# Full-height products, single PSUM banks, spectra on VectorE and a new order in a fused attention and long-convolution kernel

## The chip, the cores and the metric

The kernel runs on one core of one Trainium2 chip. The metric is device time in microseconds (us), the median of the runs shown. One execution was also taken by the hardware profiler. Its span, from the first instruction to the last, is what the rows below count from. Five engines work beside each other: TensorE (PE for its products, PEld for the loads of its stationary operand), VectorE (DVE), ScalarE (ACT), GpSimd (POOL) and SyncE (SP), which here only issues DMAs.

## What is computed

Two independent results stand side by side in an output of 2,048 rows and 1,152 columns, all in bf16. The left 576 columns are attention with a memory (32 heads of 18), in four segments of 512 rows:

```python
q, k, v = heads(x @ wq), heads(x @ wk), heads(x @ wv)
g = sigmoid(beta)                      # one per head
for s in range(4):                     # segments of 512 rows
    p = softmax(q[s] @ k[s].T * scale + causal_mask)
    a_dot = p @ v[s]
    num = phi(q[s]) @ M                # phi(t) = t + 1 where t > 0, else exp(t)
    den = phi(q[s]) @ z + 1e-6
    out[s] = g * num / den + (1 - g) * a_dot
    M, z = M + phi(k[s]).T @ v[s], z + phi(k[s]).sum(rows)
a = out @ wo
```

The right 576 columns are a gated long convolution of 2,048 taps, which the reference computes by Fourier transforms of 4,096 points:

```python
kv = short_conv(k, shift_k) * v        # 4 taps
y = irfft(rfft(pad(kv)) * rfft(pad(ssm_k)))[:2048]
b = q * (y + kv * ssm_D)
```

## The kernel before

**A list of operations and an order.** The kernel is recorded as a list of operations (`Graph.add`, L75): a name, the engines that could take it, a function that issues its instructions, the buffers that it reads and writes. Three tables at the end of the file then fix everything: `TURN` gives the order in which the operations are issued, `ENGINE` the engine of each, `SLOT` the slot of the pool in which its buffer lies. So on each engine the instructions stand in one order that is written out in full, and an instruction that waits holds all behind it on its engine. The helper `mm` issues TensorE's products (L139 without a position in the array, L141 with one), `copy` the evacuations (L145 on ScalarE, L147 on VectorE). PSUM has 8 banks of 512 fp32 columns; a buffer "ps1" is one bank, "ps2" two neighbours.

**Attention, per segment s.** x is loaded transposed (`x0`: channels 0 to 511 as four blocks of 128, `x4`: channels 448 to 575, so that the last 64 channels lie on rows 64 to 127 of the fifth block), and a copy on chip (`x5`) puts these 64 also on rows 0 to 63. Operations `qk`: for five groups of columns (four of 126, one of 72) and for q and k, four products over 128 channels each; then the last 64 channels of q and of k as two products of 64 rows that run side by side in the upper and the lower half of the array (`tile_position`). Both results lie in one pair of banks and one instruction of 1,024 elements evacuates it (`eqk`). `v` works alike with 288 columns per half, `dq` makes one head group directly in its padded form. Then come scores (L1122, 25 or 18 rows, four row tiles), exponentials on ScalarE (L1129, 1,024 elements each, 160 of them), causal masks on GpSimd (L1136), `av` (32-column tiles), division (L1207, L1208, L1236), the memory term (feature maps `phm` L936, `pha` L948; `nm` L1032), their sum `oo` (L1245, on VectorE or GpSimd) and the output products `out` with `wo` into a pair of banks, evacuated together (576 elements). In the last segment the fourth group of columns (m = 3) is cut at row 54, and its two parts are two products.

**Convolution, in five groups of 64 or 128 channels.** A short convolution by diagonal matrices `dg` (X times dg, into a pair of banks), times v (L433), then a Fourier transform in two stages of small products: `F1` (tiles W and xs, 128 rows by 64 columns, two side by side), `F2` (A and Ft), then the product of the spectra `PP` (L540: X times Hx into PQ, 1,024 elements each, one half of them on VectorE, the other on GpSimd), inverse products `inv` (G and PQ), the evacuation `Z`, a transposing DMA (`zt`, CT from Z), a last stage (`CT,Psi`) and the gate (L595, q).

**The end.** The last scores, the inverse products of channel group 4, its Z copies, their transposing DMA, its last stage and the last output products share the engines at the end of the order.

Of the kernel before, what the change touches and what calls it, by code (L numbers as in the profile page):

```python
# [18 lines left out]
P = 128  # L19
# [10 lines left out]
NDIRECT = 1  # L30
LAT = {"PE": 0.20, "ACT": 0.10, "DVE": 0.10, "POOL": 0.12, "SP": 0.10}
# [10 lines left out]
def c_tt2(n):  # L42
    return 0.16 + n * 0.00054
# [68 lines left out]
class Prog:  # L112
# [138 lines left out]
    def build_b_front(self):  # L251
# [141 lines left out]
        for ct in range(5):  # L393
# [24 lines left out]
            g.add("dg%d" % ct, {"DVE": 0.8, "POOL": 1.2}, dgf, r=[self.ident, self.skf], w=[dg, (kT, 0)], prio=pr - 2)  # L418
            for cp in range(2):
                pc = Buf("ps2", "psconv")  # L420
                for u in range(2):
                    def cm(e, pc=pc, u=u, cp=cp, kT=kT, dg=dg):
                        o = self.ps(pc)
                        c = 2 * cp + u
                        for i in range(4):
                            self.mm(o[:, u, :], self.t(dg)[:, i, :], self.t(kT)[:, 16 + 512 * c - i:16 + 512 * c - i + 512],
                                    i == 0, i == 3)

                    self.pe("conv%d.%d%d" % (ct, cp, u), 2048, 4, cm, [kT, dg], [(pc, u)], pr)

                def ce(e, pc=pc, cp=cp, vT=vT, kv=kv):
                    sl = slice(1024 * cp, 1024 * cp + 1024)
                    self.nc.vector.tensor_tensor(out=self.t(kv)[:, sl], in0=self.psf(pc), in1=self.t(vT)[:, sl], op=ALU.mult)  # L433

                self.evac("kv%d.%d" % (ct, cp), 1024, ce, [pc], [vT], pr, "D")
# [13 lines left out]
    def build_b(self):  # L449
        g, p = self.g, self.p  # L450
        for gi, (c0, Cg) in enumerate(GROUPS):
# [49 lines left out]
            for o in range(16 // KP):  # L501
# [33 lines left out]
                for ri in range(2):  # L535
# [7 lines left out]
                    g.add("PP%d.%d%d" % (gi, o, ri), {"DVE": c_tt2(1024), "POOL": c_pool2(1024)}, pa, r=[Xt, H], w=[(Pt, ri)], prio=to)  # L543
# [63 lines left out]
    def build_a_consts(self):  # L607
# [3 lines left out]
        for nm, src, lead in (("wq", "A_wq", 0), ("wk", "A_wk", 0.1), ("wv", "A_wv", 4), ("wo", "A_wo", 40)):  # L611
# [3 lines left out]
            if nm != "wo":  # L615
                cuts = (0, D) if nm == "wv" else (0, 160, D)
                qs = CQ if nm == "wv" else WQ
                for ci in range(len(cuts) - 1):
                    def l1(e, b=b, src=src, cl=slice(cuts[ci], cuts[ci + 1])):
                        self.q(e).dma_start(out=self.t(b)[:, 0:4, cl], in_=getattr(self, src)[0:512, cl].rearrange("(t p) f -> p t f", p=P))  # L620

                    self.dma(nm + "abc"[ci], l1, [], [(b, "abc"[ci])], pr + 0.3 * ci, 512 * 1152, pk=1152, queues=qs)
                for k in (["q", "k"].index(nm[1]),) if nm != "wv" else (0, 1):
                    fs = slice(288 * k, 288 * k + 288) if nm == "wv" else slice(0, D)

                    def l2(e, b=b, src=src, r=slice(64 - 64 * k, 128 - 64 * k), fs=fs):
                        self.q(e).dma_start(out=self.t(b)[r, 4, fs], in_=getattr(self, src)[512:576, fs])

                    self.dma(nm + "4%d" % k, l2, [], [(b, 1 + k)], pr + 0.2, 64 * 1152, pk=1152, queues=qs)
# [166 lines left out]
    def direct(self, hp, u, pd, xT):  # L796
        pr = self.tA(2 * hp + u) - self.p["lead_pad"] - 2
        pq = Buf("ps2", "psdq")
        for w_ in range(2):
            def dq(e, w_=w_):  # L800
                o = self.ps(pq)
                x = self.t(xT)
                for t in range(4):
                    w = self.t(self.w[("wq", "wk")[w_]])
                    for j in range(4):
                        c = DH * (8 * hp + 4 * u + j)
                        self.mm(o[32 * j:32 * j + 32, w_, :], w[:, t, c:c + 32], x[:, t, :], t == 0, False, (0, 32 * j))
                if w_ == 1:
                    for j in range(4):
                        c = DH * (8 * hp + 4 * u + j)  # L810
                        for i in range(2):
                            r = slice(64 - 64 * i, 128 - 64 * i)
                            w = self.t(self.w[("wq", "wk")[i]])
                            self.mm(o[32 * j:32 * j + 32, i, :], w[r, 4, c:c + 32], x[r, 4, :], False, True, (64 - 64 * i, 32 * j))

            ks = ("a",) if hp == 0 else ("a", "b")
            wt = self.w[("wq", "wk")[w_]]
            self.pe("dq%d.%d%d" % (hp, u, w_), 2560, 20, dq, [(xT, 0)] + [(wt, k) for k in ks] if w_ == 0 else
                    [xT, (self.w["wq"], 1), (self.w["wk"], 2)] + [(wt, k) for k in ks], [(pq, w_)] if w_ == 0 else [pq], pr, al=[pd])
        self.evac("ed%d.%d" % (hp, u), 1024, lambda e: self.copy(e, self.t(pd)[:, u, :, :], self.ps(pq)), [pq], [(pd, u)], pr + 0.5)  # L820

    def build_a(self):
# [18 lines left out]
        g.add("zz", {"POOL": 1.7}, lambda e: self.nc.gpsimd.memset(self.t(zz)[:, 0:1792], 0.0), w=[zz], prio=p["prio_w"] - 40)  # L841
        for i in range(2):
# [9 lines left out]
        for s in range(4):  # L852
# [12 lines left out]
            def lx5(e, xT=xT):  # L865
                self.nc.sync.dma_start(out=self.t(xT)[0:64, 4, :], in_=self.t(xT)[64:128, 4, :])

            self.dma("x4_%d" % s, lx4, [], [(xT, 4)], px, L * 256, pk=4096, issue=0.65, lat=2.2)
            self.dma("x0_%d" % s, lx, [], [(xT, 0)], px + 0.02, L * 1024, pk=4096, issue=0.65, lat=2.2)
            self.dma("x5_%d" % s, lx5, [], [(xT, 4)], px + 0.04, 65536, pk=1024)  # L870
            dense, f = [], []
            for m in range(5):
                M = MS[m]
                pr = ts - p["lead_qk"] + p["d_qk"] * m
                pq = Buf("ps2", "psqk")
                de = Buf("dn", "dense")
                dense.append(de)
                for w_ in range(2):
                    wt = self.w[("wq", "wk")[w_]]

                    def qk(e, pq=pq, w_=w_, wt=wt, m=m, M=M, xT=xT):
                        o = self.ps(pq)
# [555 lines left out]
```

## Time and profile before

| | |
|---|---|
| median of 3 runs | 304.22 us (300.54 to 307.75) |
| profiled execution | 303.91 us |
| span of the profiled execution | 302.2 us |
| mean granted clock of TensorE | 0.98 of full |
| busy: TensorE, VectorE, ScalarE, GpSimd | 268.0, 239.1, 240.1, 183.6 us |

The busy time of TensorE holds its products only. Its products are pipelined: the next may start before the one before has ended, so times of a group are read best from one start to the next. In a row of the timeline the bracket tells how long the engine was idle just before and what ended it. A row "x32" is 32 instructions in a run. The chain that ended last is followed back from the last instruction, at each step to what released it. PEclk, in the windows, is the granted clock as a share of full speed (1.00 is 2.4 GHz, 0.50 is 1.2 GHz).

### The profile page before, as it was taken

The page shows a single profiled execution, that of the slowest core. Times are in us where ns is not written, and L with a number is a line of the kernel's source. Part 1 is how long each engine was busy: PE and PEld are TensorE (multiplying, and loading weights), DVE is VectorE, ACT ScalarE, POOL GpSimd, SP SyncE. Part 2 cuts the span into 40 slices and gives each one's busy share as a digit, 9 for nine tenths or more (in the row PEclk, how much of TensorE's full clock was granted, in tenths as well). Part 3 has the DMA queues.
Part 4 walks back from the last instruction along what each step waited for, and adds up shares of the span by engine and source line. Part 5 has one row for each costly group of instructions (what it writes and reads, how often), then busy time and mean ns, then how long its engine had stood idle before and what let it go on. Part 6 is the DMA issues. An engine that isn't in the chain of part 4 may idle for free.

```text
span 302.2 us, 9484 instructions
## 1 busy us (share of the span) xinstructions
PE 268.0 (89%) x3978; PEld 159.7 (53%) x3978; DVE 239.1 (79%) x334; ACT 240.1 (79%) x270; POOL 183.6 (61%) x196
## 2 busy tenths in 40 slices
PE   2999999978998987999999898999989867877985
PEld 0435565445645554664655475555755534544852
DVE  6896764889999989665989889587978988789541
ACT  3277888989896896879998998889999878986621
POOL 8898043365793495082799934588757498539300
PEclk9999999999999999899999999999999999997798
DMA  8699999999999999468979556295984365783364
GB/s 201 140 184 261 163 210 326 192 205 240 237 177 233 245 128 188 107 162 141 251 153 253 128 164 164 93 230 151 235 166 127 105 171 156 166 205 87 61 96 106
DMA packets 133012, 52.92 MB, mean 175 GB/s; under 512 B 113338, under 2 KB 125738, under 8 KB 132970
## 3 DMA queue, kind: packets, MB, share of 16 engines
q1 hardware_dynamic: 130698, 51.00, 76.7%
q10 hardware_dynamic: 2272, 1.33, 1.7%
q8 instruction: 31, 0.51, 0.7%
q14 instruction: 11, 0.09, 0.1%
HBM read 21.58 MB, written 17.76 MB: 130 GB/s over the span
## 4 chain that ended last, share of the span: by engine, by line
PE 48%; DVE 17%; DMA 15%; ACT 7%; issue 7%; POOL 3%; SPq 2%; ACTq 0%; DVEq 0%; POOLq 0%
PE PS L139 23%; PE PS L141 19%; DMA CT<-Z 8%; ACT P L1129 5%; PE PS L1122 5%; DMA xs<-in_B_ssm_k_dram 4%; DVE Hx L147 2%; POOL P L1136 2%; DVE PQ L540 1%; DMA skb<-in_B_shift_k_dram 1%; DMA pad<-qk_scratch 1%; DVE X L147 1%; DVE Z L147 1%; DVE X L433 1%; DVE xs L326 1%
## 5 line engine op out<-in xcount | busy, mean ns | idle before, releaser
L1129 ACT ACTIVATE P<-PS 128x1024 bf16<-128x1024 f32 x160 | 153.4, 1032 | 24.0 <-PE PS L1122 23.8
L1136 POOL TENSOR_SCALAR_AFFINE_SELECT P<-P 128x512 bf16<-128x512 bf16 (+1 forms) x112 | 82.1, 756 | 70.5 <-ACT P L1129 56.0
L540 POOL TENSOR_TENSOR PQ<-X,Hx 128x1024 bf16<-128x1024 bf16 x18 | 41.0, 2287 | 7.7 <-DVE X L147 6.5
L1122 PE MATMUL PS<-pad 25*128 25x384 bf16 (+6 forms) x512 | 35.6, 302 | 7.6 <-DVE q L595 1.9
L936 POOL TENSOR_SCALAR f<-dn 126x512 bf16<-126x512 bf16 (+1 forms) x9 | 24.7, 2743 | 14.3 <-DVE dn L147 9.5
L139 PE MATMUL PS<-wo,am 126*128 126x288 bf16 (+2 forms) x152 | 24.9, 298 | 1.6 <-POOL am L1245 1.1
L1122 PEld LDWEIGHTS <-pad 25*128 25x128 bf16 (+1 forms) x512 | 11.0, 92 | 28.4 <-issue 23.6
L147 DVE CAST A<-PS 128x1024 bf16<-128x1024 f32 x17 | 20.6, 1216 | 6.4 <-PE PS L141 6.4
L141 PEld LDWEIGHTS <-Ft 128*64 128x64 bf16 x704 | 20.3, 110 | 8.9 <-issue 7.6
L141 PE MATMUL PS<-W,xs 128*64 128x128 bf16 x576 | 22.1, 223 | 2.8 <-ACT P L1129 1.2
L141 PE MATMUL PS<-A,Ft 128*64 128x128 bf16 (+1 forms) x640 | 22.6, 216 | 2.1 <-DVE Hx L147 0.7
L141 PE MATMUL PS<-G,PQ 64*128 64x128 bf16 (+1 forms) x640 | 23.4, 229 | 0.5 <-ACT A L145 0.4
L141 PE MATMUL PS<-P,V 128*32 128x256 bf16 (+3 forms) x512 | 22.9, 302 | 0.5 <-ACT P L1129 0.4
L139 PE MATMUL PS<-xT,wq 128*126 128x512 bf16 (+1 forms) x80 | 22.1, 403 | 1.1 <-DVE X L433 0.6
L147 DVE CAST dn<-PS 126x1024 bf16<-126x1024 f32 (+1 forms) x14 | 17.1, 1218 | 7.4 <-PE PS L141 4.0
L141 PEld LDWEIGHTS <-PQ 64*128 64x128 bf16 (+1 forms) x640 | 20.5, 105 | 4.0 <-issue 2.6
L141 PEld LDWEIGHTS <-xs 128*64 128x64 bf16 x576 | 18.1, 111 | 8.2 <-issue 7.6
L145 ACT CAST A<-PS 128x1024 bf16<-128x1024 f32 x19 | 19.2, 1016 | 3.8 <-PE PS L141 3.5
L139 PE MATMUL PS<-xT,wk 128*126 128x512 bf16 (+1 forms) x80 | 21.4, 390 | 0.0
L540 DVE TENSOR_TENSOR PQ<-X,Hx 128x1024 bf16<-128x1024 bf16 x18 | 21.2, 1186 | 0.0
L139 PE MATMUL PS<-wv,xT 128*128 128x288 bf16 x128 | 20.3, 288 | 0.6 <-ACT P L1129 0.4
L139 PE MATMUL PS<-X,dg 128*128 128x512 bf16 x80 | 19.0, 380 | 0.2 <-DVE pad L147 0.2
(149 smaller groups left out, 474.0 us busy)
## 6 DMA issues: line engine op xcount, KB each, us to landing
pad<-qk_scratch SPq DMA_DIRECT2D x15, 512.0 KB
qk_scratch<-dn SPq DMA_DIRECT2D x16, 252.0 KB
a_scratch<-ou SPq DMA_DIRECT2D x15, 256.0 KB
xs<-in_B_ssm_k_dram SPq DMA_DIRECT2D x4, 512.0 KB
kv_scratch<-X SPq DMA_DIRECT2D x4, 512.0 KB
xs<-kv_scratch SPq DMA_DIRECT2D x4, 512.0 KB
q<-in_B_q_dram SPq DMA_DIRECT2D x8, 256.0 KB
out_dram<-q SPq DMA_DIRECT2D x8, 256.0 KB
```

What stands on the lines that cost most here:

```text
L139: self.nc.tensor.matmul(out, lhsT=lhsT, rhs=rhs, start=start, stop=stop)
L141: self.nc.tensor.matmul(out, lhsT=lhsT, rhs=rhs, start=start, stop=stop, tile_position=pos)
L145: self.nc.scalar.copy(out=out, in_=in_)
L147: self.nc.vector.tensor_copy(out=out, in_=in_)
L326: v.tensor_scalar(out=self.i32(ix), in0=self.i32(it), scalar1=self.t(self.bcol)[:, 0:1], scalar2=self.t(off)[:, 0:1], op0=ALU.mult, op1=AL ...
L433: self.nc.vector.tensor_tensor(out=self.t(kv)[:, sl], in0=self.psf(pc), in1=self.t(vT)[:, sl], op=ALU.mult)
L540: eng.tensor_tensor(out=self.t(Pt)[:, 1024 * ri:1024 * ri + 1024].rearrange("p (b f) -> p b f", b=2), in0=a, in1=self.t(H)[:].rearrange("p ...
L936: eng.tensor_scalar(out=self.t(fm)[0:M, ws, :], in0=self.t(dense[m])[0:M, ws, :], scalar1=0.0, scalar2=1.0, op0=ALU.max, op1=ALU.add)
L1122: nc.tensor.matmul(o, lhsT=t[r, 1, q0:q0 + P], rhs=t[r, 0, q0:L], start=True, stop=True, tile_position=(32 * j, 0))
L1129: self.nc.scalar.activation(out=out2(jj), in_=self.psf(pso[jj]), func=ACT.Exp, scale=scale)
L1136: self.nc.gpsimd.affine_select(out=ap, in_=ap, compare_op=ALU.is_ge, fill=0.0, base=0, pattern=pat + [[1, P]], channel_multiplier=-1)
```

## The change

**Full-height products.** The weights of q, k and v get a fifth block of 128 rows: rows 64 to 127 hold the last 64 channels, rows 0 to 63 are set to zero by a memset (operations `wqz`, `wkz`, `wvz`). A product over that block has 128 rows; what x holds on rows 0 to 63 of its fifth block meets zeros. The pairs of 64-row products go, and so do the copy `x5` and the second loads of the weights' last rows.

```diff
             def lx4(e, xT=xT, s=s):
                 self.nc.sync.dma_start_transpose(out=self.t(xT)[:, 4, :], in_=self.A_x[0, L * s:L * s + L, 448:576])
 
-            def lx5(e, xT=xT):
-                self.nc.sync.dma_start(out=self.t(xT)[0:64, 4, :], in_=self.t(xT)[64:128, 4, :])
-
             self.dma("x4_%d" % s, lx4, [], [(xT, 4)], px, L * 256, pk=4096, issue=0.65, lat=2.2)
             self.dma("x0_%d" % s, lx, [], [(xT, 0)], px + 0.02, L * 1024, pk=4096, issue=0.65, lat=2.2)
-            self.dma("x5_%d" % s, lx5, [], [(xT, 4)], px + 0.04, 65536, pk=1024)
...
+                    def qk(e, pq=pqs[w_], wt=wt, m=m, M=M, xT=xT):
-                        for t in range(4):
-                            self.mm(o[0:M, w_, :], self.t(wt)[:, t, 126 * m:126 * m + M], x[:, t, :], t == 0, False)
-                        if w_ == 1:
-                            for i in range(2):
-                                w = self.t(self.w[("wq", "wk")[i]])
-                                r = slice(64 - 64 * i, 128 - 64 * i)
-                                self.mm(o[0:M, i, :], w[r, 4, 126 * m:126 * m + M], x[r, 4, :], False, True, (64 - 64 * i, 0))
...
+                        for t in range(5):
+                            self.mm(self.psf(pq)[0:M], self.t(wt)[:, t, 126 * m:126 * m + M], x[:, t, :], t == 0, t == 4)
+
+                    self.pe("qk%d.%d%d" % (s, m, w_), 2560, 5, qk, [xT, (wt, 1), (wt, 2)] + [(wt, k) for k in ks], [pqs[w_]], pr, al=[de])
+
+                for w_ in range(2):
+                    def eq(e, pq=pqs[w_], de=de, M=M, w_=w_):
+                        self.copy(e, self.t(de)[0:M, w_, :], self.psf(pq)[0:M])
+
+                    self.evac("eqk%d.%d%d" % (s, m, w_), 512, eq, [pqs[w_]], [(de, w_)], pr + 0.5)
```

The rest of that part, for the weights:

```diff
+                def l2(e, b=b, src=src):
+                    self.q(e).dma_start(out=self.t(b)[64:128, 4, :], in_=getattr(self, src)[512:576, :])
+
+                self.dma(nm + "4", l2, [], [(b, 1)], pr + 0.2, 64 * 1152, pk=1152, queues=WQ if nm != "wv" else CQ)
+                g.add(nm + "z", {"DVE": 0.4, "POOL": 0.7}, lambda e, b=b: (self.nc.vector if e == "DVE" else self.nc.gpsimd).memset(
+                    self.t(b)[0:64, 4, :], 0.0), w=[(b, 2)], prio=pr - 5)
```

**Single banks.** `qk`, `v`, `dq`, the short convolution and `out` write single banks, and each bank has its own evacuation (512 or 288 elements instead of 1,024 or 576). The waits of `phm`, `phe` and the scores name the half that they need.

**Spectra and sums on VectorE.** All 36 products of spectra (now L541), all sums `oo` and the diagonals `dg` are VectorE's. In the last segment `oo` covers m = 3 as well (its 54 rows are added into the memory term), so that the separate output product of 54 rows goes. Five more of the `phm` are GpSimd's (14 instead of 9).

```diff
-                    g.add("PP%d.%d%d" % (gi, o, ri), {"DVE": c_tt2(1024), "POOL": c_pool2(1024)}, pa, r=[Xt, H], w=[(Pt, ri)], prio=to)
+                    g.add("PP%d.%d%d" % (gi, o, ri), {"DVE": c_tt2(1024)}, pa, r=[Xt, H], w=[(Pt, ri)], prio=to)
...
-                if p["o_pool"]:
-                    en["POOL"] = c_pool2(512)
                 if mem:
-                    def o2(e, nb=nm_[s, m], b=am[m], M=M):
-                        eng = self.nc.vector if e == "DVE" else self.nc.gpsimd
-                        eng.tensor_tensor(out=self.t(b)[0:M], in0=self.t(b)[0:M], in1=self.t(nb)[0:M], op=ALU.add)
-
-                    g.add("oo%d.%d" % (s, m), en, o2, r=[nm_[s, m]], w=[am[m]], prio=pr)
+                    back = M < MS[m]
+
+                    def o2(e, nb=nm_[s, m], b=am[m], M=M, to=nm_[s, m] if back else am[m]):
+                        self.nc.vector.tensor_tensor(out=self.t(to)[0:M], in0=self.t(b)[0:M], in1=self.t(nb)[0:M], op=ALU.add)
+
+                    g.add("oo%d.%d" % (s, m), en, o2, r=[am[m] if back else nm_[s, m]], w=[nm_[s, m] if back else am[m]], prio=pr)
...
-                early = early[:3] + [(nm_[s, 3], wo, 3, MS[3]), (nm_[s, 4], wo, 4, MS[4]), (am[3], wo, 3, 54)]
+                early = early[:3] + [(nm_[s, 3], wo, 3, MS[3]), (nm_[s, 4], wo, 4, MS[4])]
```

**Warm-up products.** 18 operations of two products each, 128 rows by 512 columns, whose result nobody reads: identity times a zeroed tile (`warma`, ten), identity times `selb` (`warmb`, eight).

```diff
+        def warm(e, pw, rhs):
+            for i in range(2):
+                self.mm(self.psf(pw), self.t(self.ident)[:], rhs(), True, True)
+
+        for k in range(NWARM[0]):
+            pw = Buf("ps1", "psw")
+            self.pe("warma%d" % k, 1024, 2, lambda e, pw=pw: warm(e, pw, lambda: self.t(zz)[:, 0:512]), [self.ident, zz], [pw], p["prio_w"] - 39)
+        for k in range(NWARM[1]):
+            pw = Buf("ps1", "psw")
+            self.pe("warmb%d" % k, 1024, 2, lambda e, pw=pw: warm(e, pw, lambda: self.t(self.selb)[:, 0, 0:512]), [self.ident, self.selb], [pw],
+                    tA(34))
```

**Order.** `TURN`, `ENGINE` and `SLOT` are new; one line of `TURN`, before and after:

```diff
-    "bQBTAFUAWAAAAIMAbwAfAGwACAABAFQAVgAeAG4ACwAMAAIAVwAcAF4AAwAEAAUACQAgAHIAIwCGAIQAhwBzACEAZQAKAB0AcAAiAFoAWQANAGcABwAOAA8AhQB0AIgAJwAkACUAEAARAH8AjwCQAH"
...
+    "cwAAAHQAiwB5AIoAHAB7AHwAdQB2AGQAXwBgAF0AHgBjAB8AAQAIAAkAAgBhAGIACgALAGoAXgAhAAwAIABnAHgADQBlAIwAZgCnACMAqQClAA4ApgAiAKsAqACOAKoAEgDcAA8AEwCQAJEAEACsAA"
```

By the new tables VectorE evacuates 21 of the 40 `qk` halves (14 of 20 pairs before), 18 of 32 `v` halves (13 of 16 pairs) and 23 of 32 `out` halves (12 of 16 pairs), ScalarE the others. Seven of the warm-up operations stand at TensorE's start, four behind its last output product, seven in between. The weights' columns beyond 160 are loaded from SyncE's queue instead of ScalarE's.

On TensorE, the end of one group of columns of q and k in segment 0 and the short convolution behind it (wq and wk are the weights, xT_113 the transposed x, dg_112 the diagonals, X_0_99 the padded k). Before:

```order
L139 LDWEIGHTS wk
L139 MATMUL PS<-xT_113,wk 126x512
L141 LDWEIGHTS wq
L141 MATMUL PS<-xT_113,wq 126x512
L141 LDWEIGHTS wk
L141 MATMUL PS<-xT_113,wk 126x512
L139 LDWEIGHTS dg_112
```

The two products at L141 are the 64-row pair; ahead of them stand four products at L139 each for q and k. In the new order the fifth block's product of q follows its other four directly, and that of k too (left out are four more pairs of rows of wk):

```order
L140 LDWEIGHTS wq
L140 MATMUL PS<-xT_113,wq 126x512
L140 LDWEIGHTS wk
L140 MATMUL PS<-xT_113,wk 126x512
...
L140 LDWEIGHTS dg_112
L140 MATMUL PS<-X_0_99,dg_112 128x512
```

All rows there have one form, with no change of the array's form between q, k and the convolution.

On VectorE, the end of the work on channel group 4 of the convolution (Hx and X are its spectra, PQ their product, q the gate of group 3, am and nm the two terms of the attention). Before:

```order
L147 CAST Hx_2_107<-PS_63 128x1024
L595 TENSOR_TENSOR q_0_102<-PS_63,q_0_102 128x1024
L540 TENSOR_TENSOR PQ_0_110<-X_1_109,Hx_1_106 128x1024
L595 TENSOR_TENSOR q_0_102<-PS_63,q_0_102 128x1024
L1236 TENSOR_TENSOR am_0_134<-PS_63,am_0_134 126x512
L540 TENSOR_TENSOR PQ_1_111<-X_0_108,Hx_2_107 128x1024
L1032 TENSOR_TENSOR nm_1_141<-PS_63,rd_1_146 126x512
```

After:

```order
L541 TENSOR_TENSOR PQ_1_111<-X_1_109,Hx_0_105 128x1024
L148 CAST oA_1_150<-PS_63 128x288
L148 CAST ou_1_148<-PS_63 128x512
L541 TENSOR_TENSOR PQ_0_110<-X_0_108,Hx_2_107 128x1024
L148 CAST oA_0_149<-PS_63 128x288
L541 TENSOR_TENSOR PQ_1_111<-X_1_109,Hx_0_105 128x1024
L596 TENSOR_TENSOR q_0_102<-PS_63,q_0_102 128x1024
L541 TENSOR_TENSOR PQ_0_110<-X_0_108,Hx_2_107 128x1024
L596 TENSOR_TENSOR q_0_102<-PS_63,q_0_102 128x1024
```

All four products of the group's spectra stand on VectorE, and three of them ahead of the first gate of group 3, where before two stood here and none ahead of it.

On GpSimd, its last instructions (P4 are the exponentials that it masks). Before:

```order
L1136 AFFINE_SELECT P4_2_131<-P4_2_131 128x4x128
L540 TENSOR_TENSOR PQ_0_110<-X_1_109,Hx_1_106 128x1024
L540 TENSOR_TENSOR PQ_1_111<-X_0_108,Hx_2_107 128x1024
L1136 AFFINE_SELECT P4_3_132<-P4_3_132 128x4x128 x2
L1245 TENSOR_TENSOR am_0_134<-am_0_134,nm_2_142 126x512
L1136 AFFINE_SELECT P4_4_133<-P4_4_133 128x4x128
L1245 TENSOR_TENSOR am_1_135<-am_1_135,nm_0_140 126x512
```

After:

```order
L1123 AFFINE_SELECT P4_4_133<-P4_4_133 128x4x128
L1123 AFFINE_SELECT P4_0_129<-P4_0_129 128x4x128 x2
L1123 AFFINE_SELECT P4_1_130<-P4_1_130 128x4x128
L1123 AFFINE_SELECT P4_2_131<-P4_2_131 128x4x128
L1123 AFFINE_SELECT P4_3_132<-P4_3_132 128x8x128
L1123 AFFINE_SELECT P4_4_133<-P4_4_133 128x4x128 x2
```

Only masks are left there: two products of spectra and two sums have moved to VectorE.

## Rows read from the trace of the kernel before

**Rows 1.** Page, part 1: engine, busy us, share of the span, instructions.

```profile
PE 268.0 (89%) x3978; PEld 159.7 (53%) x3978; DVE 239.1 (79%) x334; ACT 240.1 (79%) x270; POOL 183.6 (61%) x196
```

**Rows 2.** Windows: stretch, us, PE, PEld, DVE, ACT, POOL, PEclk, DMA, GB/s.

```profile
20.00:60.00 40.00, 39.13 (x491) 21.66 (x490) 27.93 (x42) 33.74 (x39) 17.09 (x26) 1.00 1.08 234
60.00:240.00 180.00, 166.54 (x2609) 101.17 (x2607) 152.37 (x200) 158.34 (x179) 116.77 (x107) 0.99 0.81 180
240.00:302.20 62.20, 48.33 (x772) 30.84 (x769) 42.58 (x53) 40.70 (x47) 31.90 (x35) 0.93 0.55 127
```

**Rows 3.** Page, part 5: the exponentials of the scores on ScalarE.

```profile
L1129 ACT ACTIVATE P<-PS 128x1024 bf16<-128x1024 f32 x160 | 153.4, 1032 | 24.0 <-PE PS L1122 23.8
```

**Rows 4.** Timeline of TensorE: start us, us, engine line op tile.

```profile
31.81 1.05 PE L139 MATMUL PS<-xT,wk 128*72 128x512 bf16 x4
32.80 0.40 PE L141 MATMUL PS<-xT,wq 64*72 64x512 bf16 x1
32.80 0.40 PE L141 MATMUL PS<-xT,wk 64*72 64x512 bf16 x1
33.13 1.08 PE L141 MATMUL PS<-W,xs 128*64 128x128 bf16 x31
```

**Rows 5.** Timeline of TensorE, GpSimd, ScalarE: the start, [idle before <-releaser].

```profile
5.75 1.90 PE L141 MATMUL PS<-xT,wq 128*32 128x512 bf16 x16 [5.75 <-DMA xT<-in_A_x_dram]
7.58 3.21 PE L139 MATMUL PS<-xT,wq 128*126 128x512 bf16 x8
...
12.43 1.61 POOL L841 MEMSET P<- 128x1792 bf16 x1
...
23.70 1.92 ACT L1129 ACTIVATE P<-PS 128x1024 bf16<-128x1024 f32 x2
```

**Rows 6.** Timeline of VectorE, and one row of GpSimd.

```profile
56.89 0.68 DVE L540 TENSOR_TENSOR PQ<-X,Hx 128x1024 bf16<-128x1024 bf16 x1
57.49 0.68 DVE L147 CAST ou<-PS 128x512 bf16<-128x512 f32 x1
...
65.08 2.36 DVE L540 TENSOR_TENSOR PQ<-X,Hx 128x1024 bf16<-128x1024 bf16 x1
...
154.88 3.63 POOL L936 TENSOR_SCALAR f<-dn 126x1024 bf16<-126x1024 bf16 x1 [0.37 <-DVE dn L147]
...
157.66 0.68 DVE L948 TENSOR_TENSOR f<-f,fe 126x1024 bf16<-126x1024 bf16 x1
```

**Rows 7.** Groups by line and form: busy us, mean ns | idle before.

```profile
L540 POOL TENSOR_TENSOR PQ<-X,Hx 128x1024 bf16<-128x1024 bf16 x18 | 41.0, 2287 | 7.7 <-DVE X L147 6.5 <-PE PS L141 0.9 <-ACT X L145 0.3
...
L540 DVE TENSOR_TENSOR PQ<-X,Hx 128x1024 bf16<-128x1024 bf16 x18 | 21.2, 1186 | 0.0
...
L948 DVE TENSOR_TENSOR f<-f,fe 126x1024 bf16<-126x1024 bf16 x8 | 9.1, 1134 | 0.0
```

**Rows 8.** Timeline of TensorE: three waits.

```profile
118.45 0.62 PE L141 MATMUL PS<-CT,Psi 128*64 128x512 bf16 x4 [2.23 <-DMA CT<-Z]
...
248.13 0.55 PE L139 MATMUL PS<-wo,am 72*128 72x288 bf16 x3 [1.13 <-POOL am L1245]
...
276.78 0.62 PE L1122 MATMUL PS<-pad 25*128 25x512 bf16 x4 [1.94 <-DVE q L595]
```

**Rows 9.** Windows, columns as in rows 2: behind two waits.

```profile
118.50:123.00 4.50, 4.50 (x38) 2.55 (x38) 2.85 (x4) 2.02 (x3) 0.00 (x0) 0.62 0.85 226
276.50:283.20 6.70, 6.42 (x95) 5.26 (x96) 4.54 (x7) 4.43 (x5) 4.63 (x6) 0.50 0.43 81
```

**Rows 10.** Chain that ended last: start us, us, what.

```profile
270.14 0.64 PE PS L141 x4
...
278.01 3.55 PE PS L141 x64
...
286.70 7.34 DMA CT<-Z
...
294.70 3.45 PE PS L139 x22
```

More of the change, by code (lines that the diff above doesn't have):

```diff
@@ L937, in f1 @@
                                                  op0=ALU.max, op1=ALU.add)
-                g.add("phm%d.%d" % (s, m), {"DVE": c_ts4(n), "POOL": c_pool1(n)}, f1, r=[dense[m]], w=[fm], prio=pr)
+                g.add("phm%d.%d" % (s, m), {"DVE": c_ts4(n), "POOL": c_pool1(n)}, f1, r=[(dense[m], k) for k in range(ws.start, ws.stop)], w=[fm], prio=pr)
                 def f2(e, fe=fe, m=m, M=M, ws=ws, dense=dense):
                     self.nc.scalar.activation(out=self.t(fe)[0:M, ws, :], in_=self.t(dense[m])[0:M, ws, :], func=ACT.Exp)
-                g.add("phe%d.%d" % (s, m), {"ACT": c_act(n)}, f2, r=[dense[m]], w=[fe], prio=pr)
+                g.add("phe%d.%d" % (s, m), {"ACT": c_act(n)}, f2, r=[(dense[m], k) for k in range(ws.start, ws.stop)], w=[fe], prio=pr)
                 def f3(e, fm=fm, fe=fe, M=M, ws=ws):
@@ L1125, in score @@
                     cols = sum(L - P * kt for kt, _, _ in which)
-                    g.add(nm, {"PE": cols / 2400.0 + 0.05 * len(which) + 0.03}, sc, r=[(pds, k) for k in sorted({x[2] for x in which})], w=pso, prio=pr, mode="R32", al=[self._pw])
+                    g.add(nm, {"PE": cols / 2400.0 + 0.05 * len(which) + 0.03}, sc, r=[(pds, 2 * k + q) for k in sorted({x[2] for x in which}) for q in range(2)], w=pso, prio=pr, mode="R32", al=[self._pw])
                     for jj in range(2):
@@ L1214, in build_a @@
                 keys = [k for k in splits if k[0] * 4 <= hh]
-                mem = s > 0 and M == MS[m]
+                mem = s > 0
                 K = 16 * keys[-1][1]
@@ L1266, in build_a @@
-                for h in range(2):
-                    self.pe("out%d.%d%d" % (s, tt, h), 1440, 5, lambda e, h=h, op_=op_, ks=early, last=not late: op_(e, h=h, ks=ks, last=last),
-                            [x[0] for x in early] + [wo], [(po, h)], pr, al=[oA])
-                if late:
-                    def fl(e, op_=op_, late=late):
-                        for h in range(2):
-                            op_(e, h=h, ks=late, first=False)
-                    self.pe("outf%d.%d" % (s, tt), 1152, 4, fl, [x[0] for x in late] + [x[1] for x in late], [po], pr + 0.1, al=[oA])
```

214 lines of the change are left out of this document (97 added, 117 removed).

## The prediction

> **What bounds the kernel now.** I read the page's busy shares first, then the same shares by stage, then the costliest groups of instructions with what they wait for, then single stretches of the timeline and, for the end, the chain that ended last. The shares put TensorE first with 89%, VectorE and ScalarE at 79%, GpSimd at 61% [rows 1]. By stage [rows 2]: from 20 to 60 us TensorE is busy 39.1 of 40 us, from 60 to 240 us it is busy 166.5 of 180 (VectorE 152.4, ScalarE 158.3), and in the last 62.2 us only 48.3. So there are three stages: a start in which TensorE has nothing to do for 5.75 us, a long middle in which TensorE paces and the others wait for it (ScalarE's exponentials wait 23.8 us for scores [rows 3]), and an end in which it is idle a fifth of the time. The middle can shorten only if TensorE's own work shrinks or a wait in front of it goes; the end follows its chain of waits.
>
> A busy TensorE is not all products. In the timeline [rows 4] four 512-column products take from 31.81 to 32.80, 0.99 us; at the upper clock, 2.4 GHz, 512 columns are 0.213 us, four are 0.85. The pair of 64-row products behind them, side by side, is 0.213 us of columns and takes until 33.13, 0.33. So each time the array's form changes, 0.12 to 0.14 us pass beyond the columns, a little of it for the products themselves; I take 0.10 us per change. In the program's order on TensorE I count 351 changes of form before.
>
> **The change part by part.**
>
> *Products and forms.* The 64-row pairs become 128-row products. For q and k that is one more product in each of 20 pairs, 20 x 0.213 = 4.3 us; for v 16 x 288 columns (0.120 us) = 1.9; for the directly made head pair 16 products run four instead of eight at once, 0.4. Eight 54-row products of the last output stage go: 8 x 0.120 = -1.0. Sum +5.6. Against that the order has 277 changes instead of 351, and the 54-row products cost two each as well (16): 90 fewer, 90 x 0.10 = -9.0. For q and k alone it is nearly even: a pair with its two changes took 0.33 + 0.1, two full products take 0.43; v gains 0.08 each.
>
> Row tiling for contractions of at most 64 rows is what the Trainium skill recommends (TensorEngine Tiling (Array Packing), When to Use Tiling); by it alone this edit would be a loss of the 6.2 us above for q, k and v. The same page says that a change of mode drains the array (Key Properties) but gives no price. The trace has both: the two halves do start together at 32.80, and the next form starts 0.33 us later, not 0.21.
>
> Of the 18 warm-up pairs, seven stand at the start, four behind the last output product, and seven in the order between: 14 x 0.213 = +3.0 us that count. Products, forms and warm-ups: +5.6 - 9.0 + 3.0 = -0.4; I take 0. If a change cost nothing it would be +8.6; at 0.157 us each, -5.5.
>
> *Start.* Before, the first products wait for the transposed x until 5.75 us, and from 7.58 eight 512-column products then need 3.21 us, 0.40 us each [rows 5]: nearer to the 0.427 us of the lower level, 1.2 GHz, than to 0.213. Now the warm-ups need the zero tile (1.61 us on GpSimd [rows 5]) and the identity, now first on GpSimd, so they may start near 3 us (an estimate) and 14 of them at 0.427 end near 9. By 10.7 us the old kernel has done 12 steps of 512 columns, 2.6 us at full clock; the new one would have 1.7 and no copy of x to wait for. I take 0, from -2 to +2. The weights' zero rows are memsets on an idle VectorE.
>
> *Spectra and additions to VectorE.* 18 products of spectra at 0.60 us (56.89 to the next start at 57.49 [rows 6]) are +10.8 us on VectorE, 8 more additions of 512 elements some 3. What goes is what GpSimd's own two-input products did to it: alone this product takes 0.68 us, at 65.08, beside GpSimd's, 2.36; the 18 have a mean of 1.186 [rows 7], so 18 x 0.51 = 9.1 us go, and the 8 minima of 1,024 (mean 1.134 [rows 7] against 0.68 at 157.66) give 3.6, the rest about 1. VectorE stays even, at about 239 us. Split evacuations (0.68 us for 512 elements, at 57.49) cost a little more in pairs and free a bank sooner. GpSimd loses 18 x 2.29 [rows 7] and seven additions, about 50 us, gets five more feature maps (up to 3.63 us each), and its masks no longer queue behind a 2.3 us product. On the path I see two of these waits: output products at 248.13 wait 1.13 us for GpSimd's addition, and the scores at 276.78 wait 1.94 us for VectorE [rows 8]; the second belongs to the end.
>
> The Trainium skill would have the blocking differently (SBUF — State Buffer, Who interferes with whom): a VectorE instruction with two SBUF inputs contends with any GpSimd instruction that reads SBUF, and the one that came second is blocked throughout. The trace agrees for GpSimd's products, but at 157.66 a minimum took 0.68 us inside a GpSimd feature map of 3.63 us [rows 6]. If the rule decided, the masks, which stay, would block the 36 products: the slower rival below.
>
> *The middle's waits.* The largest is 2.23 us at 118.45, for the transposed spectra of group 0 [rows 8], and the clock falls behind it (0.62 over 118.5 to 123 us [rows 9], 4.5 x 0.38 = 1.7 us lost). In the new order more of TensorE's work stands between that group's last inverse product and its use, by about 12 us counted in columns and changes. I count half of the 3.9 us: -2.0 (0 to -3.9), as the in-order queue may meet another wait. The wait for GpSimd's addition: -1.0 (0 to -1.1). Together -3.0.
>
> *The end.* From the last stage of group 3 at 270.14 to the last transposing DMA at 286.70 pass 16.5 us [rows 10]. In it stand the 1.94 us wait for VectorE [rows 8] and 64 inverse products in 3.55 us at half clock (granted 0.50 from 276.5 to 283.2 [rows 9]). Now group 4's second-stage products stand ahead of that point, its spectra are four times 0.6 us on VectorE, one inverse group stands ahead of the last scores, and three instead of four follow. What is left behind that point on TensorE, counted in columns and changes, is about 8.2 us, on ScalarE six exponentials and four copies of about 0.96 (1.92 for two [rows 5]), 9.6; with the way to the last copy some 11 us instead of 16.5: -5.5. Then comes the same transposing DMA of 7.34 us, and behind it the last output products (3.45 us [rows 10]) are eight fewer: -1.0. Sum -6.5; at least the 1.94 us, at most -8.
>
> *Sum.* 0 + 0 + 0 - 3.0 - 6.5 = -9.5. The profiled execution took 303.9 us (span 302.2 and 1.7 around it): 294.4. It lies 0.3 under the median of 304.2; so 294.7.
>
> **The rivals.**
>
> 1. *VectorE is blocked and becomes the bound (slower).* If GpSimd's masks and maps stretch the 36 products to the old mean of 1.19 us, VectorE gets 18 us more than I count. From 60 to 240 us it is busy 85%; with about 15 of the 18 us falling there at the same idle share, and half the gain of the end lost, 303.9 + 15 - 3 = about 315. It decides from a mean above some 0.95 us. For it: the 2.36 us at 65.08. Against: that was beside a two-input product, which GpSimd no longer has. Chance 0.13.
> 2. *TensorE paces and the waits move (no change).* The products and warm-ups added are real, the form changes partly hide under waits anyway, and each removed wait turns into one for a PSUM bank. For it: 39.1 of 40 us busy early, no margin. The end's safest 2 us remain: about 302. Chance 0.23.
> 3. *ScalarE's stream starts earlier and carries through (faster).* The first exponentials stand at 23.70 us [rows 5]; the new order has the first scores behind five groups of products and one of transposes, which by their columns would be near 15. If the exponentials pace, 7 us more come off: 287. Against: in 20 to 60 us TensorE had no idle time to give. Chance 0.17.
>
> **How the numbers follow.** The forecast, 290 to 299 us, has 0.47. A measurement of this kernel tells about 2% from no change, that is 298 and 310 us. Faster: rival 3 and nearly all of the forecast, 0.62; slower: rival 1 and a little of the unknown price of forms, 0.14; the same: 0.24. The range goes from 284 (rival 3 with the end's full gain) to 306 (forms at no price, +8.6, against the end's gain, and the noise between runs): 13 in 100 lie beyond it in rival 1, some 5 elsewhere.
>
> **What would show it.** Right: VectorE's spectra products near 0.7 us on average and GpSimd near 140 us busy; the stretch from group 3's last stage to the last transposing DMA at about 11 us; the granted clock at 1.00 there; TensorE's form changes still 0.1 us apart; no wait over 1 us near 118. Wrong: a VectorE mean near 1.2 us (rival 1), an unchanged pace of the exponentials between 60 and 240 us with new waits for banks (rival 2), or an end that is not shorter although its stalls are gone.

## The result

The changed kernel took 284.68 us (median of 4 runs, 284.29 to 291.33), the kernel before 305.64 us (4 runs, 300.54 to 307.75): a ratio of 0.941, with a 95% interval of 0.927 to 0.955. The forecast of 294.7 us had the direction and most of the mechanism, and the time lies in the stated range of 284 to 306 us, but at its lower end: of the profiled execution's 302.2 us of span, 19.6 went, where the sum had 9.5.

The shares of the profile after, as in [rows 1], and three stretches of its span, as in [rows 2]:

```profile
PE 264.4 (94%) x4006; PEld 164.0 (58%) x4006; DVE 237.8 (84%) x403; ACT 242.7 (86%) x299; POOL 146.4 (52%) x166
```

```profile
20.00:60.00 40.00, 37.34 (x453) 22.46 (x451) 25.13 (x46) 32.64 (x44) 26.44 (x34) 1.00 1.08 219
60.00:240.00 180.00, 175.45 (x2793) 110.52 (x2793) 164.27 (x264) 172.76 (x210) 98.03 (x99) 1.00 0.82 185
240.00:282.60 42.60, 36.46 (x640) 23.96 (x632) 32.12 (x49) 28.95 (x36) 12.34 (x17) 0.98 0.78 161
```

VectorE and ScalarE did the same work as before within 3 us. What changed is how densely it stands: from 60 to 240 us VectorE is busy 164.3 us against 152.4, ScalarE 172.8 against 158.3, TensorE 175.5 against 166.5. How far the kernel has come by when is seen best in the exponentials, 160 in either kernel. The windows of that one line (columns: stretch, us, ScalarE's busy time with the number of exponentials, granted clock, DMA, GB/s), before:

```profile
20.00:60.00 40.00, 15.41 (x17) 1.00 1.08 234
60.00:120.00 60.00, 35.27 (x37) 1.00 1.06 207
120.00:180.00 60.00, 35.80 (x38) 0.98 0.72 171
180.00:240.00 60.00, 37.64 (x39) 1.00 0.64 162
240.00:302.00 62.00, 29.24 (x32) 0.93 0.56 128
```

and after:

```profile
20.00:60.00 40.00, 15.73 (x16) 1.00 1.08 219
60.00:120.00 60.00, 38.48 (x40) 1.00 1.00 211
120.00:180.00 60.00, 35.51 (x37) 1.00 0.82 187
180.00:240.00 60.00, 44.75 (x47) 1.00 0.64 157
240.00:282.60 42.60, 20.47 (x22) 0.98 0.78 161
```

From 180 to 240 us 47 exponentials were done where 39 were before; at 240 us 22 are left instead of 32. In times of single steps, read off the two timelines:

| step | before | after | gained by then |
|---|---|---|---|
| first exponential | 23.70 | 22.47 | 1.2 |
| 51st | 114.43 | 112.71 | 1.7 |
| 101st | 198.38 | 190.92 | 7.5 |
| 131st | 241.94 | 230.94 | 11.0 |
| 160th, the last | 278.42 | 262.77 | 15.7 |
| last transposing DMA issued | 286.70 | 266.84 | 19.9 |
| end of the span | 302.2 | 282.6 | 19.6 |

So some 10 us came from the middle, between the first exponential and the 131st, where the forecast had 2 (the third of its 3 is a wait at 248 us, behind that); 9 from there to the last DMA; and nothing behind it.

On TensorE I split the time from the first product to the last, from all its products' starts: columns at 2.4 GHz (what runs side by side counted once), changes of form at 0.096 us, and the rest, which is waits and low clock. Before, 292.7 us were 201.9 of columns, 35.2 for 367 changes (the 351 counted in the order and 16 of the 54-row products), and 55.6 of rest. After, 274.6 us are 215.2 (7.7 of them warm-ups), 26.6 for 277 changes, and 32.8 of rest. The columns grew by 13, and still the time fell by 18: the rest is where it came from.

### The profile page after: what moved, and what is told of

It reads as the page before. It is cut to its first block, busy times and chain, and to the rows that moved or that the text cites. A ratio compares the mean times of both kernels' runs of the same rounds, so it can differ in the third digit from the quotient of the medians.

```text
span 282.6 us, 9626 instructions
## 1 busy us (share of the span) xinstructions
PE 264.4 (94%) x4006; PEld 164.0 (58%) x4006; DVE 237.8 (84%) x403; ACT 242.7 (86%) x299; POOL 146.4 (52%) x166
## 4 chain that ended last, share of the span: by engine, by line
PE 67%; DVE 11%; ACT 8%; DMA 6%; issue 4%; POOL 1%; SPq 0%; DVEq 0%; ACTq 0%; POOLq 0%
PE PS L140 36%; PE PS L142 23%; PE PS L1109 8%; ACT P L1116 6%; DMA qk_scratch<-dn 3%; DMA xT<-in_A_x_dram 2%; DVE xs L327 2%; DVE dg L416 1%; PE PS L1033 1%; DMA am<-a_scratch 1%; DVE am L1223 1%; DVE dn L148 1%; DVE q L596 1%; DVE Mbd L1077 1%; ACT A L146 1%
## 5 line engine op out<-in xcount | busy, mean ns | idle before, releaser
L928 POOL TENSOR_SCALAR f<-dn 126x1024 bf16<-126x1024 bf16 (+3 forms) x14 | 42.4, 3027 | 13.9 <-PE PS L140 6.8
L140 PE MATMUL PS<-xT,wk 128*126 128x512 bf16 (+1 forms) x100 | 25.3, 384 | 1.7 <-DMA xT<-in_A_x_dram 1.6
L148 DVE CAST A<-PS 128x1024 bf16<-128x1024 f32 x19 | 23.1, 1219 | 4.4 <-PE PS L142 4.1
L140 PE MATMUL PS<-xT,wq 128*126 128x512 bf16 (+1 forms) x100 | 25.3, 383 | 0.6 <-DVE Hx L148 0.6
L541 DVE TENSOR_TENSOR PQ<-X,Hx 128x1024 bf16<-128x1024 bf16 x36 | 24.8, 698 | 0.3 <-PE PS L142 0.3
L140 PE MATMUL PS<-wv,xT 128*128 128x288 bf16 x160 | 23.3, 286 | 0.1
L140 PE MATMUL PS<-wo,am 126*128 126x288 bf16 (+1 forms) x144 | 22.4, 287 | 0.3 <-DVE oA L148 0.3
L148 DVE CAST dn<-PS 126x512 bf16<-126x512 f32 (+1 forms) x21 | 14.4, 684 | 9.6 <-DMA qk_scratch<-dn 4.9
L148 DVE CAST X<-PS 128x1024 bf16<-128x1024 f32 x15 | 18.3, 1222 | 3.2 <-PE PS L142 2.5
L140 PEld LDWEIGHTS <-xT 128*128 128x128 bf16 x160 | 14.7, 98 | 6.8 <-issue 2.4
```

The source lines that it names most:

```text
L140: self.nc.tensor.matmul(out, lhsT=lhsT, rhs=rhs, start=start, stop=stop)
L148: self.nc.vector.tensor_copy(out=out, in_=in_)
L541: eng.tensor_tensor(out=self.t(Pt)[:, 1024 * ri:1024 * ri + 1024].rearrange("p (b f) -> p b f", b=2), in0=a, in1=self.t(H)[:].rearrange("p ...
L928: eng.tensor_scalar(out=self.t(fm)[0:M, ws, :], in0=self.t(dense[m])[0:M, ws, :], scalar1=0.0, scalar2=1.0, op0=ALU.max, op1=ALU.add)
```

## The experiments

Ratios are to the kernel before in the same series of runs, with 95% intervals; its own median lay between 300.9 and 304.0 us in them.

**What the parts bring alone, in the old order.** First, the engine of the spectra and of the sums:

```diff
-        o.eng = ENGS[eng[o.i]]
+        o.eng = "DVE" if o.name[0:2] in ("PP", "oo") else ENGS[eng[o.i]]
```

> The kernel before, with all products of spectra and all sums on VectorE, in the old order. Theory (the change of engine by itself takes the stalls away): VectorE's busy time stays near 239 us, the mean of the products falls from 1.19 to 0.7, and the time falls by 4 to 9 us against the kernel before (304 to 306). Rival (only the new order can use it: in the old one twice as many products queue on VectorE ahead of what TensorE waits for): between -2 and +4 us.

It took 298.92 us: 0.994 (0.989 to 0.998), 2 us less than before: less than the theory, and at the edge of the rival. The stalls are gone in full (the group of products of spectra, as in [rows 7]):

```profile
L540 DVE TENSOR_TENSOR PQ<-X,Hx 128x1024 bf16<-128x1024 bf16 x36 | 24.4, 689 | 0.0
```

Yet the time hardly follows. Second, the full-height products:

```diff
-                                r = slice(64 - 64 * i, 128 - 64 * i)
-                                self.mm(o[0:M, i, :], w[r, 4, 126 * m:126 * m + M], x[r, 4, :], False, True, (64 - 64 * i, 0))
+                                self.mm(o[0:M, i, :], w[:, 4, 126 * m:126 * m + M], x[:, 4, :], False, True)
```

and likewise for v, with memsets that zero the other half of the weights.

> The kernel before, with each 64-row pair of q, k and v replaced by two full-height products over zero weights; engines, order and banks as before. Theory (a form change costs 0.096 us, and columns and changes both count in full): 6.2 us of columns more against some 60 to 70 changes less, 6 to 7 us: even, 300 to 303 us where the kernel before takes 302. Rival (the columns are hidden in the old kernel's waits and the changes are not, or the other way round): 295 to 297, or 306 to 308.

304.20 us: 1.008 (1.003 to 1.013), a loss of some 2 us. The order now has 303 changes of form instead of 351: 48 x 0.096 = 4.6 us less, against 6.2 of columns. So by columns and changes the pairs were slightly the better choice here, by 1.6 us: the price of the form change takes most of their gain away. That the choice falls to the pairs is as the Trainium skill has it (TensorEngine Tiling (Array Packing), When to Use Tiling). The measured loss is no firm proof of it: in this run's profiled execution the first exponential already stands at 27.64 us against 23.70, and only 0.8 us more are lost from there to the 131st. The run also puts four memsets on VectorE at the start. Third, all edits of the code at once, with the old tables (of a step that is now divided, both halves stand where the whole stood, in the same banks and on the same engine) and without warm-ups:

```diff
-            for i in range(2):
-                self.mm(self.psf(pw), self.t(self.ident)[:], rhs(), True, True)
+            return
```

> All edits of the code, but the old order: full-height products, single banks with split evacuations, spectra, sums and diagonals on VectorE, no warm-ups; order, banks and all other engines as in the tables of the kernel before. To be read beside the changed kernel without warm-ups (287.7). Theory (the parts by themselves bring little, the order that was built on them brings the rest): 295 to 300 us. Rival (the parts make the gain, whatever the order): 287 to 291.

299.81 us: 0.998 (0.994 to 1.002). All edits together bring nothing that can be measured, while the changed kernel without its warm-ups, which differs from this one in the tables alone, took 287.70. The theory held: some 12 us hang on the tables, that is on the order, the engines and the slots together. The windows of this run, as in [rows 2], look like those of the kernel before:

```profile
60.00:240.00 180.00, 169.81 (x2643) 106.13 (x2640) 153.72 (x258) 160.62 (x189) 83.76 (x86) 0.99 0.81 179
240.00:300.00 60.00, 44.66 (x745) 28.34 (x737) 42.14 (x65) 39.58 (x48) 18.18 (x27) 0.93 0.58 132
```

**What the parts are worth in the new order.** The same engine edit backwards: 18 products and seven sums to GpSimd again.

```diff
-        o.eng = ENGS[eng[o.i]]
+        o.eng = "POOL" if o.name in ON_POOL else ENGS[eng[o.i]]
```

> The changed kernel, but 18 products of spectra and seven sums go back to GpSimd, the same ones as in the kernel before; the order of issue stays the changed one. Theory (much of the gain is that VectorE is no longer held up beside GpSimd's two-input products, and that masks no longer queue behind them): the mean of VectorE's products of spectra rises from 0.70 to about 1.2 us, GpSimd from 146 to about 195 us busy, time 293 to 300. Rival (the order makes the gain, and the engine of the spectra is no matter): 284 to 288.

298.96 us, 14 more than the changed kernel, and 0.993 (0.989 to 0.996) to the kernel before: the new order is worth next to nothing with these operations on GpSimd. GpSimd's busy time is 193.3 us, and the products left on VectorE slow down, to 0.86 us and not to the 1.2 that was expected:

```profile
L541 POOL TENSOR_TENSOR PQ<-X,Hx 128x1024 bf16<-128x1024 bf16 x18 | 40.5, 2254 | 16.2 <-PE PS L142 7.5 <-DVE X L148 4.6 <-issue 3.0
...
L541 DVE TENSOR_TENSOR PQ<-X,Hx 128x1024 bf16<-128x1024 bf16 x18 | 15.3, 859 | 0.3 <-PE PS L142 0.3
```

Then the seven sums alone (the same edit with the sums' names only):

> The changed kernel, but only seven sums of the attention's two terms go back to GpSimd; the spectra stay on VectorE. With both back the time was 299.0. Theory (18 products of 2.25 us make most of that loss): 285 to 288 us. Rival (the sums stand directly ahead of the output products, and their 1.2 to 2.1 us behind masks cost as much): 291 to 295.

286.80 us, 2 more than the changed kernel: the 18 products make most of the 14. Then the form changes, by letting the fifth product of each q, k and v group use the lower half of the array, alone:

```diff
-                            self.mm(self.psf(pq)[0:M], self.t(wt)[:, t, 126 * m:126 * m + M], x[:, t, :], t == 0, t == 4)
+                            r = slice(0 if t < 4 else 64, 128)
+                            self.mm(self.psf(pq)[0:M], self.t(wt)[r, t, 126 * m:126 * m + M], x[r, t, :], t == 0, t == 4, None if t < 4 else (64, 0))
```

> The changed kernel, but the fifth product of each q, k and v group has 64 rows in the lower half of the array, alone and not in a pair: same columns, same order, only the array's form changes ahead of it and behind it, some 144 times more. Theory (a change of form costs about 0.1 us of TensorE's time, and TensorE is on the path): +10 to +14 us, 295 to 299. Rival (the changes hide beside waits): below +3, up to 288.

294.77 us, 10.1 more than the changed kernel. In the order these are 104 changes more (381 for 277, as some neighbours had another form anyway): 0.097 us each, the 0.096 that the gaps in the trace of before give. On a TensorE with 94% of the span, a change of form was paid in full.

**Warm-ups.** Without all 18, by the edit of `warm` shown above, the order as changed:

> The changed kernel without its 18 warm-up operations (36 products that nobody reads); all else, the order too, as changed. Theory (the warm-ups are TensorE work of 7.7 us, of which half stands in the order between other work, and the clock does not depend on them): 281 to 285 us, against 284.7 with them. Rival (they keep the clock up and the start warm): without them the first 10 us run at the lower clock and stretches of granted clock near 0.5 come back behind the waits, as at 118 and 276 us before: 287 to 291 us.

287.70 us (287.40 to 288.51), 3 more: the time is the rival's, but not by the start. The first products run slowly without them (five in 2.8 us instead of 1.2), but they start at 6.81 us, where the warm-ups hold them until 8.39; the first exponential stands at 22.48 us against 22.47. Behind two waits the low clock came back, in the windows of that run, columns as in [rows 2]:

```profile
48.50:52.20 3.70, 3.40 (x25) 1.64 (x27) 0.69 (x1) 0.60 (x2) 1.34 (x3) 0.56 1.07 341
240.00:243.40 3.40, 3.40 (x29) 1.38 (x28) 1.91 (x4) 2.94 (x4) 1.27 (x3) 0.51 0.70 140
```

and in the changed kernel:

```profile
48.50:52.20 3.70, 3.44 (x49) 2.01 (x50) 1.29 (x2) 2.11 (x3) 1.58 (x3) 1.00 0.94 328
240.00:243.40 3.40, 3.23 (x55) 1.95 (x51) 3.26 (x5) 3.40 (x5) 1.84 (x3) 1.00 0.75 148
```

In the same time TensorE does 25 products instead of 49, and 29 instead of 55. TensorE's timeline shows the first place, without warm-ups:

```profile
48.80 2.32 PE L140 MATMUL PS<-xT,wk 128*126 128x512 bf16 x5 [1.87 <-DMA xT<-in_A_x_dram]
```

and with them:

```profile
48.76 1.29 PE L140 MATMUL PS<-xT,wk 128*126 128x512 bf16 x5 [1.60 <-DMA xT<-in_A_x_dram]
```

The wait for x is there in both, but with warm-ups the granted clock stays at 1.00. What keeps it there is not shown: between 8.6 and 50.3 us no warm-up stands in the changed kernel's order, so none is near this wait, which is also shorter there (1.60 us against 1.87). Of the inner seven, three pairs stand at 50.31, 55.67 and 58.32 us, behind it; only the pair at 233.78 us stands ahead of the second place.

Nor is the low clock the whole loss. The exponentials of the run without warm-ups lag by 0.2 us at the 21st (67.89 against 67.69) and still at the 41st, by 1.6 at the 101st (192.55 against 190.92) and the 131st, and by 2.9 at the last (265.69 against 262.77). So about half of the lag arose behind the wait at 240 us, and half between the 41st and the 101st exponential, where the granted clock of both is 1.00 (the line is that of the run without warm-ups, columns as in [rows 2]):

```profile
60.00:240.00 180.00, 174.10 (x2766) 109.96 (x2764) 163.66 (x262) 171.41 (x209) 98.62 (x98) 1.00 0.84 184
```

And one of the four executions without warm-ups had the clock at 1.00 throughout and was the longest, 288.51 us.

To see which of them count, the seven at the start and the four at the end were left out:

```diff
+            if nm in ('warma0', 'warma5', 'warma7', 'warma8', 'warma1', 'warma2', 'warma4', 'warmb4', 'warmb1', 'warmb0', 'warmb7'):
+                return
```

> The changed kernel with the seven warm-up operations inside the order only; the seven at TensorE's start and the four behind its last output product issue nothing. Theory (what counts is the granted clock behind two waits, near 48 and 240 us, and only the inner ones stand there; the first exponentials came at 22.47 us with and 22.48 without warm-ups): 284 to 285.5 us, as with all. Rival (the start counts: TensorE's first products run at the lower level without them): 286.5 to 288.

285.40 us (283.05 to 286.90): not to be told from the 284.68 with all. The seven in the order are enough; how they bring their 2 to 3 us stays open in part. Warm-ups are no guard of the clock either: the two runs with all 18 and with products or sums back on GpSimd have 0.50 from 17.5 to 20.5 us and from 270.1 to 273.2.

**What in the tables.** The new order with the old engines of the copies and feature maps, and the reverse: the first differs from the changed kernel, the second from the run that took 299.81 us, in the table of engines alone.

> The changed kernel with its new order, but every evacuation and feature map on the engine that the kernel before has for it (some 80 operations change between VectorE and ScalarE, nine between GpSimd and VectorE). Theory (the order of the steps makes the gain; who copies matters little): 285 to 290 us. Rival (order and engines were fitted to each other, and either alone is lost): 294 to 300.

> All edits of the code in the old order, as in the run that gave 299.8 us, but every evacuation and feature map on the engine that the changed kernel has for it. Theory (the order of the steps makes the gain): 298 to 302 us. Rival (the division of copies between VectorE and ScalarE makes it): 288 to 294.

They took 325.81 us (1.080, 1.069 to 1.090) and 343.03 us (1.129, 1.112 to 1.146). My theory fell in both, and the rivals were far too mild: against the same order with its own engines, either lost 14% (325.81 to 284.68, 343.03 to 299.81). Each of the two orders needs the engines it was made with. The shares of the first and of the second:

```profile
PE 276.7 (86%) x3990; PEld 170.1 (53%) x4006; DVE 243.4 (75%) x420; ACT 241.7 (75%) x287; POOL 127.1 (39%) x161
```

```profile
PE 277.6 (81%) x3963; PEld 170.7 (50%) x3970; DVE 240.4 (70%) x406; ACT 242.4 (71%) x296; POOL 144.5 (42%) x166
```

The busy times of VectorE and ScalarE are within 6 us of those of the fast kernel; for the rest of the time they wait. In the first, the exponentials wait for scores 19.6 us, in the second 35.0, in the changed kernel 7.7.

**The forecast's wait at 118 us.** In the old order, the last stage of group 0 and its gate were moved 24 and 17 operations of TensorE later (tables alone):

> The kernel before with one step of its order moved: the last stage of channel group 0 and its gate stand 24 and 17 operations of TensorE later, so that its transposing DMA has time to land. Theory (the forecast's term: the 2.23 us wait at 118 us and half the 1.7 us of clock behind it are on the path): -2 to -4 us. Rival (what TensorE does not wait there it waits a few products on, since ScalarE and VectorE set the pace in that stretch too): -1 to +1.

306.42 us: 1.012 (1.001 to 1.022). The expected gain did not come. The wait for the DMA is gone, but another of the same length stands in its place. The timeline of that run, TensorE, then VectorE and GpSimd:

```profile
119.87 0.40 PE L1122 MATMUL PS<-pad 25*128 25x512 bf16 x4 [2.19 <-DVE A L147]
...
116.09 2.59 DVE L948 TENSOR_TENSOR f<-f,fe 126x1024 bf16<-126x1024 bf16 x1
118.61 1.21 DVE L147 CAST A<-PS 128x1024 bf16<-128x1024 f32 x1
...
116.02 2.12 POOL L540 TENSOR_TENSOR PQ<-X,Hx 128x1024 bf16<-128x1024 bf16 x1
```

GpSimd's product starts at 116.02, VectorE's minimum beside it takes 2.59 us, the copy behind it (A) is late, and TensorE waits 2.19 us for that copy's bank. In the kernel before, the same minimum took 2.61 us at 114.63; the wait of [rows 8] had a second one under it. The last run had both edits, this move and the spectra on VectorE:

> The kernel before with two edits together: all products of spectra and all sums on VectorE (alone: ratio 0.994 to the kernel before), and the last stage of channel group 0 moved behind 24 and 17 further operations of TensorE (alone: 1.012, and the 2.2 us of wait for the DMA came back as 2.2 us for a bank that VectorE evacuated late, behind a minimum stretched to 2.6 us beside GpSimd's product). Theory (each of the two hides behind the other at that place, so that together they bring what neither brings alone): no wait over 1 us between 115 and 122 us, ratio 0.978 to 0.988. Rival (TensorE meets a third wait there, or loses the time in the products that follow): 0.990 to 1.005.

The ratio was 0.987 (0.978 to 0.995), better than the kernel before, but not to be told from the engine edit alone (0.989 to 0.998). At the place itself the theory held (TensorE, then VectorE):

```profile
119.36 0.40 PE L1122 MATMUL PS<-pad 25*128 25x512 bf16 x4 [0.32 <-DVE A L147]
...
117.49 0.68 DVE L948 TENSOR_TENSOR f<-f,fe 126x1024 bf16<-126x1024 bf16 x1
118.09 1.22 DVE L147 CAST A<-PS 128x1024 bf16<-128x1024 f32 x1
```

From the 51st exponential to the 61st it took 18.6 us, where the kernel before took 21.2, the engine edit alone 21.1 and the move alone 20.0: together more than the sum. But from the 51st to the 71st it was 34.4 against 34.7. Within ten exponentials the gain had gone into the next waits.

## Why the prediction was right, and where not

*Start* (forecast 0, from -2 to +2): -1.2 us at the first exponential, but the warm-ups have no part in it (22.48 without them). The start also varies between executions: in the old order the first exponential stood at 23.70 us here and at 25.12 in the run with the move, whose order differs only far behind it.

*Products and forms* (forecast 0): the columns (+5.6 us), the count and the price of a change hold. The 74 changes fewer in the order and the 16 of the 54-row products are the forecast's 90; at the 0.097 us measured they are 8.7 us, where the forecast had 9.0. That a 54-row product costs two changes, though it is given no position in the array, stands in the trace of before (TensorE):

```profile
287.20 0.41 PE L139 MATMUL PS<-wo,nm 126*128 126x288 bf16 x2
287.54 0.29 PE L139 MATMUL PS<-wo,am 54*128 54x288 bf16 x1
287.76 0.26 PE L139 MATMUL PS<-ident,ou 128*128 128x4 bf16 x4
```

Two products of 288 columns, 0.24 us of columns, take 0.34 from start to start, and the 54-row product takes 0.22 instead of 0.12: 0.10 on either side. Two things of this part were wrong. A pair was counted with two changes, 72 for the 36 pairs, but in the old order only 48 go with them, as some neighbours have another form anyway; so q, k and v alone come out as a small loss and not as even or better. And the warm-ups stand in the sum as work, +3.0: without them the kernel takes 3 us more, not less, so this term had the wrong sign.

*Spectra*: VectorE stayed even (239.1, now 237.8, forecast 239), and hardly anything but GpSimd's two-input products had stalled it. The groups, as in [rows 7]:

```profile
L541 DVE TENSOR_TENSOR PQ<-X,Hx 128x1024 bf16<-128x1024 bf16 x36 | 24.8, 698 | 0.3 <-PE PS L142 0.3
...
L940 DVE TENSOR_TENSOR f<-f,fe 126x1024 bf16<-126x1024 bf16 x8 | 5.8, 725 | 0.0
```

The 36 products take 0.698 us on average (forecast "near 0.7") beside masks and feature maps that read SBUF on GpSimd for 146 us (forecast 140). So rival 1 did not come. Six of the 36 stood wholly inside a feature map and took 0.68 to 0.69 us; the slowest two, 0.88 and 0.90 us, stood beside masks. The rule of the Trainium skill as the prediction put it (SBUF — State Buffer, Who interferes with whom) would have had them wait for maps and masks, and the trace does not agree.

*The middle's waits*: this is the step that was mis-sized most, "I count half of the 3.9 us: -2.0" and "On the path I see two of these waits", together -3.0. The middle gave some 10. The sign named for it did come: from 102 to 168 us TensorE has no wait over 0.6 us. I had priced single waits off the timeline, one by one. The run with the move shows that the first of them was worth nothing by itself, and the run with products and sums back on GpSimd that these cost 14 us in the new order, where their edit brought 2 in the old. Under the one wait that was followed up stood three constraints (a DMA, a bank, a stretched instruction), and only with all of them gone was the place free; that the other waits are alike is argued and not shown. So the direction was right for a smaller reason than the true one. Which steps of the new order carry the 12 us of the tables, and whether slots count in them beside the order, was not tried and stays open.

*The end*: from group 3's last stage to the last transposing DMA it took 16.6 us and now 9.5 (257.37 to 266.84), where the forecast had 11; the granted clock is 1.00 from 236 to 280 us. The chain in order of time, as in [rows 10]:

```profile
262.14 1.91 PE PS L142 x64
...
266.11 1.20 PE PS L142 x32
267.31 5.94 PE PS L140 x58
273.25 0.55 PE PS L142 x4
```

The 64 inverse products of [rows 10] take 1.91 us where they took 3.55, and the DMA's 6.4 us are filled with output products. Behind it the forecast's -1.0 for eight products fewer did not come. TensorE's last products are no longer what the end waits for; SyncE's queue is. Its last four issues, in the timeline:

```profile
276.26 0.64 SPq L603 DMA_DIRECT2D out_dram<-q  x1
276.96 0.65 SPq L1263 DMA_DIRECT2D out_dram<-oA  x1
277.70 0.63 SPq L603 DMA_DIRECT2D out_dram<-q  x1
278.44 0.66 SPq L1263 DMA_DIRECT2D out_dram<-f  x1
```

The gate is done at 276.23, and four issues some 0.7 us apart follow.

*The rivals*: of rival 2, no change, much was true of the parts taken alone in the old order: the products added are real work, and the one wait that was removed turned into another. Rival 3 had the time nearly right (287) for a reason that did not occur: the first exponentials came at 22.47 us, not near 15. Since the range got its lower end of 284 from that rival, it is in part luck that the measured time lies inside it.

## What to carry to other kernels

The length of a wait read off a timeline is not yet the gain: here the longest of the middle, 2.23 us, brought nothing when its cause alone was moved. Look at what the waiting engine would have met next, and at the second cause that stands under the first. Where an order is written out by hand or by a planner, price an edit together with the order that is made for it. The same edit was worth 2 us in the old order and 14 in the new, and either order with the other's engines lost 14%.

## What the runs showed of the hardware that was not expected

A change of the array's form costs 0.097 us of TensorE's time here (104 changes, 10.1 us), so that a pair of 64-row products side by side gains little over two full ones. Two such costs stood around each 54-row product too, which was given no position in the array (0.10 us on either side). Seven pairs of products that nobody reads, inside the order, brought 2 to 3 us, although only one of them stands shortly ahead of one of the two waits behind which the granted clock fell without them (to 0.56 over 3.7 us and to 0.51 over 3.4). And a minimum of 1,024 elements on VectorE took up to 2.61 us beside a two-input product on GpSimd; in the changed kernel, beside masks and maps only, it took 0.67 to 0.99.
